# Scores and V products of an attention kernel tied into one run on TensorE

## The chip, the cores and the metric

The kernel runs on one core of a Trainium2 chip. The metric is the time of one execution on the device, in microseconds (us); the median of three runs of the kernel before is 1221.32 us (1220.86 to 1222.01). A core has TensorE (PE, matmuls, with its weight loads shown apart as PEld), VectorE (DVE), ScalarE (ACT), GpSimd (POOL) and SyncE (SP, which issues DMAs). Matmul results land in PSUM and are copied from there by DVE or ACT.

## What is computed

Attention over hash buckets, then a Fourier mix with a feed-forward layer (B = 4 batches, H = 8 heads, S = 768 positions, D = 64, model width 512, hidden width 2048):

```python
q_bits = (einsum('bhsd,dk->bhsk', q, proj) > 0)          # 6 bits, k_bits alike
mask = q_bucket[:, :, :, None] == k_bucket[:, :, None, :]
scores = where(mask, scale * matmul(q, k.transpose(0, 1, 3, 2)), -1e9)
attn = softmax(scores)                                   # over the keys
x = matmul(attn, v)                                      # -> (B, S, H*D)
mixed = real(fft(fft(x, axis=1), axis=2))
u = x + mixed
un = (u - mean(u)) / sqrt(var(u) + 1e-6)
out = u + maximum(un @ w_ch1, 0) @ w_ch2
```

All matmuls of scores, V products and layers are float32.

## The kernel before, in words

**Attention.** Heads are taken two at a time: a pair `n` (0 to 15, four to a batch) has its two heads in partitions 0 to 63 and 64 to 127. `attention(b)` (L851) goes over the four pairs of a batch, and for each over six chunks `c` of 128 keys. One chunk of one pair is called a step here; a step does the following.

- `weigh(n, g, c)` (L782), once for each query half `g` (384 queries): the two heads' scores go into one PSUM tile `sc` by two matmuls (L796), each with 64 rows, one on the upper and one on the lower half of the array. ACT takes the exponential into `pk` (L802), DVE multiplies it by the bucket mask, head by head (L805). So a step has four score matmuls: half 0 head 0, half 0 head 1, half 1 head 0, half 1 head 1. The profile shows two records for each float32 matmul, eight for a step. There are two `sc` tiles and four `pk` tiles.
- DVE adds `pk` into running sums (L876), once for each half.
- `finish()` (L855) then takes the step before out of the list `pending` and calls `values` (L811): four matmuls (L816), for each half two heads, whose results lie in partitions 0 to 63 and 64 to 127 of a PSUM tile `oo`. Behind a pair's last chunk comes `scale` (L821), with the sum matmuls (L833) and the division. What is still pending at the end of a batch is finished behind the loop (L888).
- From the second chunk on, one piece of `prepare(n + 1)` (L694) is made ready: transposes of q and k (L708), hash bits (L749), and for pairs 5 to 15 the bucket numbers of queries `qb` (L761, four bfloat16 matmuls) and keys `kb` (L770, six small ones), both through `sc` tiles. Pairs 0 to 4 are "lite": they have no `kb`, and take the mask through two further matmuls for each half, which add into the same scores (L791).

**The mix.** `mix(b)` makes the Fourier transforms (L964, L993), then in two halves of the positions the hidden layer `h` (L1018, chains of four matmuls over 384 columns, then a relu on ACT or DVE), transposes `un` (L1034), and the output `o` (L1049, chains of sixteen matmuls over 512 columns, added to `u` by DVE and stored). These use the two small PSUM tiles `ps`, in turn with the transposes, bits and sums of attention.

**Order.** Batch 0's attention stands in a `manual_schedule` block (L1080), in which PE, DVE, ACT and POOL keep the written order. From batch 1 on, attention of batch `b` is written step by step, with some pieces of the mix of batch `b - 1` behind every step (L1107 to L1113); batch 3's mix comes last, alone. There the order on each engine is left to the scheduler of the framework: it plays the program through and gives an engine, of the instructions that are ready, the one that ranks first; the rank is the written order unless the program raises it. A score matmul written behind h matmuls can so be started before them, when those wait for a PSUM tile.

Of the kernel before, what the change touches and what calls it, by code (L numbers as in the profile page):

```python
# [1 line left out]

# [1 line left out]

# [6 lines left out]
F32 = mybir.dt.float32  # L11
# [8 lines left out]
P = 128  # L20
# [4 lines left out]
NT = S // P  # L25
NPAIR = H // 2
HALF = S // 2
# [451 lines left out]
def _main(  # L479
# [13 lines left out]
    nc = tc.nc  # L493
# [13 lines left out]
    def wt(shape, dtype, tag, name, bufs=2):  # L507
        return work.tile(shape, dtype, tag=tag, name=name, bufs=bufs)
# [15 lines left out]
    def evac(dst, src, act=False):  # L524

        flip[0] ^= 1
        if flip[0] and not act:
            nc.vector.tensor_copy(dst, src)  # L528
        else:
            nc.scalar.copy(dst, src)  # L530
# [37 lines left out]
    pw = const.tile([P, 2, P], BF16, tag="pw", name="pw")  # L568
# [9 lines left out]
    for i in range(NPK):  # L578
        pk = const.tile([P, 2, HALF + 1], F32, tag=f"pk{i}", name=f"pk{i}")
# [114 lines left out]
    def prepare(n):  # L694

        lite = n in LITE
        act = lite and n > 0
        ts = {}  # L700
        for io, nm in enumerate("qk"):
            tn = nat.pop((nm, n))
            tt = wt([P, S], F32, nm + "t", f"{nm}t{n}")
            for g in range(2):
                ps = pt([P, 3, P], f"tr{nm}{n}_{g}")
                for i in range(3):
                    c = 2 * i + g if nm == "q" else 3 * g + i
                    nc.tensor.transpose(  # L708
                        ps[:, i, :], tn[:, c].rearrange("p h d -> p (h d)"), ident
                    )  # L710
                if nm == "q":
                    for i in range(2):
                        dst = tt[:, i * HALF + g * HALF // 2 : i * HALF + (g + 1) * HALF // 2]
                        evac(
                            dst.rearrange("p (j c) -> p c j", c=3),
                            ps[:, :, i * D : (i + 1) * D], act,
                        )
                else:
                    evac(
                        tt[:, g * HALF : (g + 1) * HALF],  # L720
                        ps.rearrange("p c t -> p (c t)"), act,
                    )
            ts[nm] = tt
            yield
            norm(n, io, tn)
        if lite:


            qk = wt([P, 2, S], BF16, "qb", f"qkb{n}")
            for io, nm in enumerate("qk"):  # L730
                for g in range(2):
                    cols = slice(g * HALF, (g + 1) * HALF)
                    ps = pt([P, HALF], f"bits{nm}{n}_{g}")
                    nc.tensor.matmul(ps, pjw, ts[nm][:, cols], start=True, stop=True)
                    bits = qk[:, io, cols]
                    nc.vector.tensor_scalar(
                        bits, ps, 0.0, off[:, io : io + 1],
                        op0=ALU.is_gt, op1=ALU.subtract,
                    )
                    if io == 0:  # L740
                        nc.vector.tensor_scalar(bits, bits, BIG, None, op0=ALU.mult)
                yield
            preps[n] = ts["q"], ts["k"], qk, None
            return

        ps = pt([P, HALF], f"bits{n}")
        for j in range(4):
            src = ts["qk"[j // 2]][:, (j % 2) * HALF : (j % 2 + 1) * HALF]
            nc.tensor.matmul(  # L749
                ps[32 * j : 32 * j + 32, :], pj, src, start=True, stop=True  # L750
            )
        bt = wt([P, HALF], BF16, "bt", f"bt{n}")
        nc.vector.tensor_scalar(bt, ps, 0.0, None, op0=ALU.is_gt)
        yield

        qb = wt([P, 2, S], BF16, "qb", f"qb{n}")
        for h in range(2):
            ps = ps_sc.tile([P, 2, 512], F32, tag="sc", name=f"qb{n}_{h}")
            for g in range(2):
                rows = slice(32 * g, 32 * g + 32)  # L760
                nc.tensor.matmul(  # L761
                    ps[:, g, 0:HALF], pw[rows, h, :], bt[rows, :], start=True, stop=True
                )
            evac(qb[:, h, :].rearrange("p (g s) -> p g s", g=2), ps[:, :, 0:HALF])
        kb = wt([P, 2, NT], F32, "kb", f"kb{n}")
        ps = ps_sc.tile([P, 2, 512], F32, tag="sc", name=f"kb{n}")
        for c in range(NT):
            g, i = divmod(c, NT // 2)
            rows = slice(64 + 32 * g, 96 + 32 * g)
            nc.tensor.matmul(  # L770
                ps[:, g, 2 * i : 2 * i + 2], bt[rows, i * P : (i + 1) * P],
                pw[rows, :, 0], start=True, stop=True,
            )
        nc.vector.tensor_copy(
            kb.rearrange("p h (g i) -> p g i h", g=2),
            ps[:, :, 0:NT].rearrange("p g (i h) -> p g i h", h=2),
        )
        preps[n] = ts["q"], ts["k"], qb, kb

    npk = [0]  # L780

    def weigh(n, g, c):  # L782

        qt, kt, qb, kb = preps[n]
        qs = slice(g * HALF, (g + 1) * HALF)
        ks = slice(c * P, (c + 1) * P)
        ps = ps_sc.tile([P, 2, 512], F32, tag="sc", name=f"sc{n}_{g}_{c}")
        heads = [slice(h * D, (h + 1) * D) for h in range(2)]
        if kb is None:
            for h, rows in enumerate(heads):  # L790
                nc.tensor.matmul(  # L791
                    ps[:, h, 0:HALF], qb[rows, 1, ks], qb[rows, 0, qs],
                    start=True, stop=False,
                )
        for h, rows in enumerate(heads):
            nc.tensor.matmul(  # L796
                ps[:, h, 0:HALF], kt[rows, ks], qt[rows, qs],
                start=kb is not None, stop=True,
            )
        pk = pks[npk[0] % NPK]  # L800
        npk[0] += 1
        nc.scalar.activation(pk[:, :, 0:HALF], ps[:, :, 0:HALF], AF.Exp, scale=SCALE)  # L802
        if kb is not None:
            for h in range(2):
                nc.vector.scalar_tensor_tensor(  # L805
                    pk[:, h, 0:HALF], qb[:, h, qs], kb[:, h, c : c + 1], pk[:, h, 0:HALF],
                    op0=ALU.is_equal, op1=ALU.mult,
                )
        return pk

    def values(n, c, pk, oos):  # L811

        for g in range(2):
            w = HALF + 1 - g
            for h in range(2):
                nc.tensor.matmul(  # L816
                    oos[g][h * D : (h + 1) * D, 0:w], nat["v", n][:, c, h, :],
                    pk[g][:, h, 0:w], start=(c == 0), stop=(c == NT - 1),
                )
# [31 lines left out]
    def attention(b):  # L851
        xs[b] = wt([P, NPAIR, S], F32, "x", f"x{b}")
        pending = []

        def finish():  # L855
            n, c, pk, oos, accs = pending.pop(0)
            values(n, c, pk, oos)
            if c == NT - 1:
                scale(n, oos, accs)

        for t in range(NPAIR):
            n = NPAIR * b + t
            half = fold(b, 0) if t == NPAIR - 1 else iter(())
            if 1 < n + 1 < NPAIR * B:
                load(n + 1)
            ahead = prepare(n + 1) if n + 1 < NPAIR * B else iter(())
            oos = [ps_o.tile([P, 512], F32, tag="o", name=f"oo{n}_{g}") for g in range(2)]
            accs = [wt([P, 2, HALF], F32, "t3", f"acc{n}_{g}", 4) for g in range(2)]
            first = None
            for c in range(NT):  # L870
                new = [weigh(n, g, c) for g in range(2)]
                if c == 0:
                    first = new
                else:
                    for g in range(2):
                        nc.vector.tensor_tensor(  # L876
                            accs[g], first[g][:, :, 0:HALF] if c == 1 else accs[g],
                            new[g][:, :, 0:HALF], op=ALU.add,
                        )
                while pending:  # L880
                    finish()
                pending.append((n, c, new, oos, accs))
                if c > 2:
                    next(half, None)
                if c > 0:
                    next(ahead, None)
                yield
        while pending:  # L888
            finish()

# [205 lines left out]
    for b in range(B):  # L1096
# [17 lines left out]
        if b == B - 1:  # L1114
# [6 lines left out]
            ps = pt([1, 3, P], "norms_t")  # L1121
# [65 lines left out]
```

## Time and profile before

| what | value |
|---|---|
| median of three runs | 1221.32 us |
| the profiled execution | 1220.78 us, span 1218.6 us |
| granted TensorE clock, mean | 0.994 of full speed |
| scores, L796, in all | 768 records, 187.3 us busy |
| V products, L816, in all | 768 records, 145.0 us busy |
| h, L1018, in all | 1024 records, 346.3 us busy |
| o, L1049, in all | 800 records, 339.9 us busy |
| mask multiplies, L805 | 264, 615 ns each |
| exponentials, L802 | 192, 809 ns each |

The span goes from the first to the last instruction of the profiled execution; the rest of its time lies around it. A row of a group has the line, the engine, the operation, what it writes and reads by the program's names, the shape and the count; then the busy time, the mean length of one in ns, and the idle time of the engine just before them with what ended it. A row of the timeline has the start, the length of a run of like instructions (to the end of the last, which can overlap the start of the next row), and their count; in brackets stands the engine's idle time before it. Where matmuls follow each other closely, the distance between starts is what they cost PE. A row of the waits has who waited for whom, the time in all, how often, and the longest.

### The profile page before, as it was taken

The numbers are of one execution on the slowest core, as the hardware profiler recorded it, in microseconds if no ns is written. First come the engines' busy times: TensorE is split into PE (matmuls) and PEld (weight loads), VectorE is DVE, ScalarE is ACT, GpSimd is POOL, SyncE is SP. The second block draws the span as 40 slices with busy tenths as digits, with TensorE's granted clock in tenths as the row PEclk, the third lists the DMA queues.
The fourth block names the chain that finished last, engine by engine and source line by source line (L and its number), as shares of the span: only waits on it lengthen the run. The fifth ranks groups of instructions, "written<-read, shape, count | busy, mean of one in ns | idle before, by whom it ended". The sixth has DMA issues, their size and how long they took to land. (4 is left out here: it accounts for less than half of the span.)

```text
span 1218.6 us, 11905 instructions
## 1 busy us (share of the span) xinstructions
PE 1182.9 (97%) x4617; PEld 596.3 (49%) x4617; DVE 635.4 (52%) x1202; ACT 347.0 (28%) x612; POOL 57.6 (5%) x128
## 2 busy tenths in 40 slices
PE   7999899999999999999999999999999999999997
PEld 4444364444444456454445445554445546654555
DVE  5889869753374547545446555655445753211110
ACT  7877356532132122222222213222122210000000
POOL 1000001000000010000000010000000000001001
PEclk9999999899999999999999999999999999999999
DMA  9522124201010010100101011010000000000000
GB/s 277 156 65 45 44 87 147 83 14 43 9 26 14 22 38 6 27 13 22 35 22 27 1 31 35 1 39 1 22 17 1 1 10 18 1 1 17 9 9 20
DMA packets 82896, 44.24 MB, mean 36 GB/s; under 512 B 76816, under 2 KB 76944, under 8 KB 82832
## 3 DMA queue, kind: packets, MB, share of 16 engines
q1 hardware_dynamic: 75600, 23.61, 8.0%
q0 software_dynamic: 5664, 19.40, 4.9%
q8 instruction: 38, 0.62, 0.2%
q10 hardware_dynamic: 1568, 0.39, 0.2%
q14 instruction: 26, 0.21, 0.1%
HBM read 37.10 MB, written 6.29 MB: 36 GB/s over the span
## 5 line engine op out<-in xcount | busy, mean ns | idle before, releaser
L1018 PE MATMUL h<-x,w 128*128 128x384 f32 x1024 | 346.3, 494 | 4.8 <-ACT qt L530 2.4
L1049 PE MATMUL o<-w,h 128*128 128x512 f32 (+1 forms) x800 | 339.9, 578 | 0.0
L1018 PEld LDWEIGHTS h<-x,w 128*128 128x128 f32 x1024 | 192.2, 191 | 150.8 <-issue 13.1
L805 DVE SCALAR_TENSOR_TENSOR pk<-qb,kb,pk 128x384 f32<-128x384 bf16 x264 | 151.2, 615 | 184.0 <-ACT pk L802 183.8
L1049 PEld LDWEIGHTS o<-w,h 128*128 128x128 f32 x800 | 148.3, 190 | 169.5 <-issue 160.3
L802 ACT ACTIVATE pk<-sc 128x768 f32<-128x768 f32 x192 | 148.4, 809 | 217.8 <-PE sc L796 178.7
L796 PE MATMUL sc<-qt,kt 64*128 64x384 f32 x768 | 187.3, 507 | 0.0
L816 PE MATMUL oo<-pk,vn 128*64 128x385 f32 (+1 forms) x768 | 145.0, 499 | 0.0
L876 DVE TENSOR_TENSOR acc<-acc,pk 128x768 f32<-128x768 f32 x128 | 120.4, 955 | 9.2 <-ACT pk L802 7.6
L1027 ACT ACTIVATE h<-h 128x384 f32<-128x384 f32 x64 | 31.4, 490 | 281.3 <-PE h L1018 281.2
L1025 DVE TENSOR_SCALAR h<-h 128x384 f32<-128x384 f32 x64 | 35.5, 554 | 143.0 <-PE h L1018 142.9
L796 PEld LDWEIGHTS sc<-qt,kt 64*128 64x128 f32 x768 | 76.6, 186 | 65.9 <-issue 44.3
L1055 DVE SCALAR_TENSOR_TENSOR u<-o,rs,u 128x512 f32<-128x512 f32 (+1 forms) x25 | 18.2, 729 | 165.8 <-PE o L1049 118.3
L816 PEld LDWEIGHTS oo<-pk,vn 128*64 128x64 f32 x768 | 46.6, 136 | 87.3 <-issue 82.5
L1036 ACT COPY u<-un 128x512 f32<-128x512 f32 x24 | 14.0, 586 | 127.3 <-PE un L1034 127.3
L1042 POOL TENSOR_SCALAR rs<-mv 128x1 f32<-128x1 f32 x24 | 7.7, 323 | 593.4 <-DVE mv L1040 588.4
L903 POOL DMA_DIRECT2D out_dram<-u x33 | 19.9, 603 | 316.4 <-DVE u L1055 255.7
L964 PE MATMUL cs<-ch,z 128*128 128x128 f32 (+3 forms) x192 | 31.1, 314 | 2.6 <-DVE kt L528 1.4
L964 PEld LDWEIGHTS cs<-ch,z 128*128 128x128 f32 x192 | 27.5, 191 | 10.1 <-DVE kt L528 3.1
L971 ACT COPY F<-cs 128x257 f32<-128x257 f32 (+1 forms) x32 | 11.1, 374 | 74.7 <-PE cs L964 74.7
L876 DVE TENSOR_TENSOR acc<-pk,pk 128x768 f32<-128x768 f32 x32 | 30.0, 951 | 2.0 <-ACT pk L802 1.7
L828 ACT ACTIVATE x<-oo,vs 128x384 f32<-128x384 f32 x32 | 16.8, 577 | 41.3 <-DVE vs L825 41.3
(107 smaller groups left out, 805.7 us busy)
## 6 DMA issues: line engine op xcount, KB each, us to landing
zraw<-in_moe_w_ch_dram POOLq DMA_DIRECT2D x21, 512.0 KB, 4.5
vn<-in_v_dram SPq DMA_DIRECT2D x32, 192.0 KB, 3.3
qn<-in_q_dram SPq DMA_DIRECT2D x31, 192.0 KB, 3.2
kn<-in_k_dram SPq DMA_DIRECT2D x31, 192.0 KB, 3.2
out_dram<-u POOLq DMA_DIRECT2D x15, 256.0 KB, 2.4
out_dram<-u POOLq DMA_DIRECT2D x18, 128.0 KB, 2.5
fraw<-in_moe_w_ch_dram SPq DMA_DIRECT2D x4, 512.0 KB, 9.2
fraw<-in_moe_w_ch_dram POOLq DMA_DIRECT2D x4, 512.0 KB, 4.5
```

What stands on the lines that cost most here:

```text
L796: nc.tensor.matmul(ps[:, h, 0:HALF], kt[rows, ks], qt[rows, qs], start=kb is not None, stop=True,)
L802: nc.scalar.activation(pk[:, :, 0:HALF], ps[:, :, 0:HALF], AF.Exp, scale=SCALE)
L805: nc.vector.scalar_tensor_tensor(pk[:, h, 0:HALF], qb[:, h, qs], kb[:, h, c : c + 1], pk[:, h, 0:HALF], op0=ALU.is_equal, op1=ALU.mult,)
L816: nc.tensor.matmul(oos[g][h * D : (h + 1) * D, 0:w], nat["v", n][:, c, h, :], pk[g][:, h, 0:w], start=(c == 0), stop=(c == NT - 1),)
L876: nc.vector.tensor_tensor(accs[g], first[g][:, :, 0:HALF] if c == 1 else accs[g], new[g][:, :, 0:HALF], op=ALU.add,)
L903: nc.gpsimd.dma_start(out[b, s0 : s0 + 2 * w - 1 : 2, cols], src[at : at + w, cols])
L964: nc.tensor.matmul(ps[:, pc + 2 * lo : pc + 2 * hi - 1 : 2], z[:, cp, pc, par, t * P : (t + 1) * P], ch[:, cp, pc, lo:hi], start=(cp == 0) ...
L1018: nc.tensor.matmul(ps, w1[:, c, fc * P : (fc + 1) * P], x[:, c, g * HALF : (g + 1) * HALF], start=(c == 0), stop=(c == NDC - 1),)
L1025: nc.vector.tensor_scalar(hr, ps, 0.0, None, op0=ALU.max)
L1027: nc.scalar.activation(hr, ps, AF.Relu)
L1049: nc.tensor.matmul(ps, hs[fc][:, j * P : (j + 1) * P], w2[:, fc, cols], start=(fc == 0), stop=(fc == NFC - 1),)
L1055: nc.vector.scalar_tensor_tensor(u[:, cols], ps, rs, u[:, cols], op0=ALU.mult, op1=ALU.add)
```

## The change

Two context managers are used together. `tc.issue_after(ins)` orders the matmuls made inside it behind `ins` on PE; `tc.high_priority(offset=500)` raises their rank by 500 places. `behind()` does both, behind the matmul that was noted last in `last[0]`. The rank of the first matmul of a step's scores stays as it was; the other three, each behind the one before, and then the four V products of the step before, all behind the last score matmul, are raised. This holds for batches 1 to 3 (`n >= NPAIR`), and not for the V products that are finished behind a batch's loop (`t is None`). The `qb` and `kb` matmuls are tied in the same way, and the tile `kb` is made before the `qb` matmuls instead of behind them. The instructions, their operands and the DMAs are the same.

```diff
         qb = wt([P, 2, S], BF16, "qb", f"qb{n}")
+        kb = wt([P, 2, NT], F32, "kb", f"kb{n}")
         for h in range(2):
...
-                nc.tensor.matmul(
-                    ps[:, g, 0:HALF], pw[rows, h, :], bt[rows, :], start=True, stop=True
-                )
+                with behind() if g + h else nullcontext():
+                    last[0] = nc.tensor.matmul(
+                        ps[:, g, 0:HALF], pw[rows, h, :], bt[rows, :],
+                        start=True, stop=True,
+                    )
             evac(qb[:, h, :].rearrange("p (g s) -> p g s", g=2), ps[:, :, 0:HALF])
-        kb = wt([P, 2, NT], F32, "kb", f"kb{n}")
...
+            with behind() if c else nullcontext():
+                last[0] = nc.tensor.matmul(
+                    ps[:, g, 2 * i : 2 * i + 2], bt[rows, i * P : (i + 1) * P],
+                    pw[rows, :, 0], start=True, stop=True,
+                )
...
+    AHEAD = 500
+
+    last = [None]
+
+    @contextmanager
+    def behind():
+
+        with tc.issue_after(last[0].ins), tc.high_priority(offset=AHEAD):
+            yield
...
         for h, rows in enumerate(heads):
-            nc.tensor.matmul(
-                ps[:, h, 0:HALF], kt[rows, ks], qt[rows, qs],
-                start=kb is not None, stop=True,
-            )
+            with behind() if g + h and n >= NPAIR else nullcontext():
+                last[0] = nc.tensor.matmul(
+                    ps[:, h, 0:HALF], kt[rows, ks], qt[rows, qs],
+                    start=kb is not None, stop=True,
+                )
...
             n, c, pk, oos, accs = pending.pop(0)
-            values(n, c, pk, oos)
+            with behind() if n >= NPAIR and t is not None else nullcontext():
+                values(n, c, pk, oos)
...
+        t = None
         while pending:
             finish()
```

More of the change, by code (lines that the diff above doesn't have):

```diff
@@ L1 @@
-from contextlib import ExitStack
+from contextlib import ExitStack, contextmanager, nullcontext
 import numpy as np
@@ L769, in prepare @@
             rows = slice(64 + 32 * g, 96 + 32 * g)
-            nc.tensor.matmul(
-                ps[:, g, 2 * i : 2 * i + 2], bt[rows, i * P : (i + 1) * P],
-                pw[rows, :, 0], start=True, stop=True,
-            )
+            with behind() if c else nullcontext():
[3 more added lines that the diff above has]
+                )
         nc.vector.tensor_copy(
@@ L795, in weigh @@
         for h, rows in enumerate(heads):
-            nc.tensor.matmul(
-                ps[:, h, 0:HALF], kt[rows, ks], qt[rows, qs],
-                start=kb is not None, stop=True,
-            )
+            with behind() if g + h and n >= NPAIR else nullcontext():
[3 more added lines that the diff above has]
+                )
         pk = pks[npk[0] % NPK]
```

## The prediction

> **What bounds the kernel now.** I read the page's busy line first, then the table of stages, then the waits of TensorE (PE).
>
> ```profile
> span 1218.6 us, 11905 instructions
> PE 1182.9 (97%) x4617; PEld 596.3 (49%) x4617; DVE 635.4 (52%) x1202; ACT 347.0 (28%) x612; POOL 57.6 (5%) x128
> ```
> ```profile
> 0.00:140.00 140.00, 124.76 (x658) 57.03 (x660) 112.90 (x207) 96.12 (x178) 6.49 (x28) 0.99 0.44 122
> 140.00:220.00 80.00, 74.14 (x363) 42.81 (x363) 63.58 (x125) 51.33 (x97) 7.40 (x14) 0.96 0.39 117
> 220.00:990.00 770.00, 763.09 (x2883) 370.04 (x2882) 414.16 (x776) 183.22 (x305) 29.46 (x56) 1.00 0.08 20
> 990.00:1219.00 229.00, 220.87 (x717) 126.40 (x715) 44.72 (x98) 16.29 (x34) 14.21 (x30) 0.99 0.04 11
> ```
>
> The columns after the length are busy time (and instructions) of PE, weight loads, DVE, ACT, POOL, then the granted clock. Batch 0, written out by hand, lies before 140 and is untouched; the last mix lies after 990, with no scores. The change works in 140 to 990. In 220 to 990 PE is idle for 6.9 us of 770, DVE for 356. So PE's own time sets the end there, and whatever PE no longer spends comes off the end, unless a wait appears.
>
> Is all that busy time needed? Scores (L796) and V products (L816) answer it. They have the same number of columns and the same kind of packing: two heads side by side, each on half the array.
>
> ```profile
> L796 PE MATMUL sc<-qt,kt 64*128 64x384 f32 x568 | 146.6, 516 | 0.0
> L816 PE MATMUL oo<-pk,vn 128*64 128x385 f32 x284 | 61.6, 512 | 0.0
> L816 PE MATMUL oo<-pk,vn 128*64 128x384 f32 x284 | 57.9, 486 | 0.0
> ```
>
> These are groups of 140 to 990: 568 records each way (a float32 matmul leaves two records, so one step has 8), but the scores take 146.6 us and the V products 119.5. The timeline of PE shows why.
>
> ```profile
> 594.74 0.91 PE L796 MATMUL sc<-qt,kt 64*128 64x384 f32 x2
> 595.58 7.13 PE L1049 MATMUL o<-w,h 128*128 128x512 f32 x16
> 602.65 1.55 PE L796 MATMUL sc<-qt,kt 64*128 64x384 f32 x6
> 604.13 1.51 PE L816 MATMUL oo<-pk,vn 128*64 128x385 f32 x8
> 605.57 0.52 PE L749 MATMUL bits<-qt,pj 128*32 128x384 f32 x2
> ...
> 613.42 1.56 PE L796 MATMUL sc<-qt,kt 64*128 64x384 f32 x8
> 614.91 1.51 PE L816 MATMUL oo<-pk,vn 128*64 128x385 f32 x8
> ```
>
> At 613.42 a step's scores run whole: 8 records, 1.49 us until V starts. At 594.74 the first head's matmul runs alone (2 records) and holds PE for 0.84 us until 595.58; its partner comes 7 us later, in a run of 6 that takes 1.48, as long as a whole run of 8: there the second head of half 0 shares the array with the first head of half 1, and the last head is alone. So the early piece is pure loss. The V products are never torn: 1.44 us each time.
>
> **The change, part by part.** *Lone heads.* I went along the PE timeline and sorted the 66 steps of pairs 5 to 15. 29 are whole. 26 are torn into 2 and 6 (first at 185.81, last at 976.17). 7 are in three pieces, as here:
>
> ```profile
> 410.28 0.91 PE L796 MATMUL sc<-qt,kt 64*128 64x384 f32 x2
> 411.12 0.66 PE L1034 MATMUL un<-ident,x 128*128 128x128 f32 x4
> 411.71 0.92 PE L796 MATMUL sc<-qt,kt 64*128 64x384 f32 x4
> 412.56 14.00 PE L1049 MATMUL o<-w,h 128*128 128x512 f32 x32
> ```
>
> A piece of 2 holds PE 0.84 us, a piece of 4 for 0.85. 4 steps are in two halves of 4. Whole, each would take 1.49. Saved: 26 x (0.84 + 1.48 - 1.49 = 0.83) = 21.6; 7 x (0.84 + 0.85 + 0.84 - 1.49 = 1.04) = 7.3; 4 x (2 x 0.85 - 1.49 = 0.21) = 0.8. Together 29.7 us.
>
> *Entering and leaving the packed form.* A long run of plain matmuls between plain neighbours gives the clean spacing:
>
> ```profile
> 1098.92 13.90 PE L1049 MATMUL o<-w,h 128*128 128x512 f32 x32
> 1112.66 0.60 PE L1034 MATMUL un<-ident,x 128*128 128x128 f32 x4
> ```
>
> 13.74 us for 32 records, 0.429 each. The 16 records between the two pieces at 595.58 and 602.65 took 7.07 us, where 16 x 0.429 is 6.87: each visit to packed matmuls costs the plain ones around it 0.20 us. The torn steps have 26 + 14 + 4 = 44 pieces too many; 9 pieces follow a sum matmul, whose own packed form pays this anyway. 35 x 0.20 = 7.0 us.
>
> Check against the group: 71 steps x 1.56 (a whole run's length above) = 110.8, against 146.6: 35.8 too much. My classes give 29.7 plus 44 x 0.07 (a piece's 0.91 overlaps the next by 0.07) = 32.8; the other 3 us are pair 4. There two further score matmuls per half (L791) aren't glued, only the heads: between 0 and 3 us, and I take 2, since the heads are most of it.
>
> *Waits behind torn scores.* Some pieces fill time in which PE would wait for a copy out of PSUM, and not all of it:
>
> ```profile
> PE h L1018 <- ACT qt L530: 2.4, 4, 0.6
> PE cs L964 <- ACT qt L530: 1.2, 2, 0.6
> ```
> ```profile
> 349.82 1.15 DVE L805 SCALAR_TENSOR_TENSOR pk<-qb,kb,pk 128x384 f32<-128x384 bf16 x2 [3.77 <-ACT pk L802]
> 351.69 1.55 PE L796 MATMUL sc<-qt,kt 64*128 64x384 f32 x6
> 351.88 1.14 DVE L805 SCALAR_TENSOR_TENSOR pk<-qb,kb,pk 128x384 f32<-128x384 bf16 x2
> 353.85 8.01 PE L1018 MATMUL h<-x,w 128*128 128x384 f32 x24 [0.60 <-ACT qt L530]
> ```
>
> Glued, the scores and V of this place last 1.49 + 1.44 = 2.93 us from 351.69, to 354.62, past the 353.85 at which h was free to go: these six waits (3.6 us) go under cover. Ends: 0 and 3.6; I take 3.6. The later gaps of such a step lose their filler, but the next step's run of 2.93 us can take it, since its first matmul keeps its old place.
>
> *The new wait.* The V products now come directly behind the next step's scores, and the transposes, h, o and bits matmuls queue behind them on PE; ACT and DVE (relu, copies out of PSUM, bits) wait for those. V needs the exponentials (ACT) and masks (DVE) of its own step. The tightest place is the one just shown: V would start at 351.69 + 1.49 = 353.18, and the last mask ends at 351.88 + 1.14 = 353.02. Twelve steps of pairs 5 to 15 follow the one before this closely. If V is put behind some h instead, it costs one more visit, 0.20 each, 2.4 us; if it fits, 0; if it falls apart into single heads, 2.7 each (rival 1), 32 us. I take 2.4, nearest to the row with its margin of 0.16.
>
> *The rest* costs nothing: qb and kb matmuls already run as 4 and 6 in a row; the earlier kb tile moves no instruction; no DMA is moved; batch 0 and the last V products of a batch are left as they are.
>
> *The early stage.* 140 to 220 has 5.9 us of idle PE, which I count at zero change; the low end takes it as covered, with what follows its longest wait:
>
> ```profile
> 214.20 8.15 PE L1018 MATMUL h<-x,w 128*128 128x384 f32 x15 [2.37 <-ACT kt L530]
> ```
> ```profile
> 214.00:221.00 7.00, 6.80 (x12) 3.81 (x13) 4.95 (x10) 6.61 (x14) 0.53 (x1) 0.54 0.60 185
> ```
>
> After a wait of 2.37 us the granted clock was 0.54 for 7 us, another 7 x 0.46 = 3.2 us. The Trainium skill (TensorE: Matmul & The Clock Gate, Part 1) lets the clock fall only after an idle window of about 3.4 us; by it this wait would cost nothing more and the low end would be 3 us higher. The trace contradicts that here, and a row decides.
>
> *Sum.* 29.7 + 7.0 + 2 + 3.6 - 2.4 = 39.9 us. The profiled execution took 1220.78 (span 1218.6 and 2.2 around it), 0.5 under the median of 1221.32. 1220.8 - 39.9 + 0.5 = 1181.4, so 1181.
>
> **The rivals.** *1. V waits for DVE and falls apart: slower.* The V matmuls are raised in rank one by one and not tied to each other. Where a step's run comes before the masks are done, each head may go as its mask comes, with plain matmuls between. No lone V head is in the trace; the nearest row is a lone score head, 0.84 plus 0.20 for the visit: four make 4.2 us, against 1.44 in the run, 2.7 us lost per step. The gain of 39.9 is gone from 15 steps on. At two steps of each of the 12 pairs, 24 x 2.7 = 65: 1246 us. For it: DVE's masks of half 1 wait for the half-0 sum, and only 0.16 us is to spare at 353.18. Against: only twelve steps are this close, and DVE is 54% busy (414 of 770). Chance 6%. The Trainium skill (TensorEngine Tiling, PSUM Bottleneck) warns that packing speeds TensorE and not the evacuation, which may then set the pace; this is that rule at work, and DVE's share speaks against it so far.
>
> *2. The pieces were fillers, and the waits come back.* If the next run can't take a gap, PE idles for what 353.85 shows still left, about 0.6 us, at most of the 35 plain pieces: 35 x 0.6 = 21, so 1202 us. For it: the pieces stand behind transposes and sums, which fill both small PSUM buffers. Against: the run is longer than any piece, there are 72 of them, and the 9 pieces behind sums need little (h follows at once). 10%.
>
> *3. The glue doesn't bind.* If being ordered behind a matmul isn't being next to it, the pieces stay: 1221 us. Against: accumulating matmuls, too, are only ordered one behind the other, and run unbroken: 32 records of o at 412.56, two chains of 16. 4%.
>
> **How the numbers follow.** Forecast 80%, rivals 10, 6 and 4. The forecast's own range goes from 1181 less 5.9 + 3.2, that is 1172, to 1181 plus the 5.6 of the two terms taken at their good ends and a third of rival 1's twelve steps (11), 1198. To hold rival 2, it reaches to 1204. A measurement of this kernel can tell about 0.2%, 2.4 us, from no change. Faster by more: 80 + 10 + 1 of rival 1's few-step form = 91%; within: 3; slower: 5 of rival 1 and 1 of rival 3 = 6.
>
> **What would show it.** Right: nearly every row of L796 between 140 and 990 with x8 and a V row x8 directly behind; their group at 111 to 115 us instead of 146.6, V still near 119.5; the plain matmul groups unchanged in busy time but for the visits; PE idle no more than 10 us. Wrong, by rival 1: V rows of x2 or x4, and V's group well over 120. By 2: the scores at 111, but waits of h, o and transposes on ACT or DVE above 15 us in sum. By 3: scores at 146 still. The forecast is wrong if the time is above 1204 with scores whole.

## The result, and the profile after

The changed kernel takes 1189.1 us (median of 4, 1188.4 to 1190.8) against 1221.7: a ratio of 0.974, 95% interval 0.972 to 0.975. Its profiled execution took 1188.4 us. First the page's head:

```profile
span 1186.2 us, 11922 instructions
PE 1148.7 (97%) x4617; PEld 585.8 (49%) x4617; DVE 634.2 (53%) x1202; ACT 346.0 (29%) x612; POOL 60.2 (5%) x128
```

The span is 32.4 us shorter, PE's busy time 34.2. So PE is idle for 37.5 us (span less busy), 1.8 more than before: the gain is all in PE's busy time, and waits took back a little of it. Now the groups of 140 to 990, as shown of before (busy us and mean ns, then idle us before them; L811 and L831 are the score and V lines of the changed kernel):

```profile
L811 PE MATMUL sc<-qt,kt 64*128 64x384 f32 x568 | 111.7, 507 | 0.0
L831 PE MATMUL oo<-pk,vn 128*64 128x385 f32 x288 | 64.2, 512 | 0.5 <-DVE pk L820 0.4
L831 PE MATMUL oo<-pk,vn 128*64 128x384 f32 x288 | 59.4, 487 | 0.0
```

Scores fell from 146.6 to 111.7 us for the same 568 records. V has 8 records more in this window; in the whole program V went from 145.0 to 147.0. The timeline of PE shows the runs:

```profile
641.40 0.49 PE L708 MATMUL trk<-ident,kn 128*128 128x128 f32 x3
641.82 1.56 PE L811 MATMUL sc<-qt,kt 64*128 64x384 f32 x8
643.31 1.51 PE L831 MATMUL oo<-pk,vn 128*64 128x385 f32 x8
644.75 0.55 PE L708 MATMUL trk<-ident,kn 128*128 128x128 f32 x3
645.14 7.91 PE L1035 MATMUL h<-x,w 128*128 128x384 f32 x24
652.97 0.52 PE L749 MATMUL bits<-qt,pj 128*32 128x384 f32 x2
...
653.75 5.43 PE L1035 MATMUL h<-x,w 128*128 128x384 f32 x16
```

Of the 66 steps of pairs 5 to 15, 64 have their scores whole, 2 in halves; no lone score head is left. Two things differ from what the prediction drew. The raised run cuts the six transposes of k into 3 and 3. And the bits matmuls, which in the kernel before stood right behind V (605.57 there) and shared its packed form, now stand alone between plain matmuls (652.97), another visit.

At two steps V fell apart as rival 1 has it, in the crowded stretch around 200 us:

```profile
195.17 1.56 PE L811 MATMUL sc<-qt,kt 64*128 64x384 f32 x8
196.66 2.20 PE L1035 MATMUL h<-x,w 128*128 128x384 f32 x6
198.92 0.86 PE L831 MATMUL oo<-pk,vn 128*64 128x385 f32 x2
199.71 0.91 PE L1035 MATMUL h<-x,w 128*128 128x384 f32 x2
200.55 0.86 PE L831 MATMUL oo<-pk,vn 128*64 128x385 f32 x2
201.34 0.91 PE L1035 MATMUL h<-x,w 128*128 128x384 f32 x2
202.18 0.87 PE L831 MATMUL oo<-pk,vn 128*64 128x384 f32 x4
```

A lone V head (2 records) holds PE for 0.79 us, until 199.71. Between 220 and 990 the h matmuls wait like this; the row below the waits is one of the two places:

```profile
PE h L1035 <- ACT qt L530: 2.3, 2, 1.3
PE h L1035 <- DVE h L1042: 1.1, 1, 1.1
```
```profile
352.92 1.88 PE L1035 MATMUL h<-x,w 128*128 128x384 f32 x5 [1.28 <-ACT qt L530]
```

The four waits of h of 0.6 us are gone, but two longer ones of the same kind (up to 1.3 us) came with the cut transposes: their second half, and so its copies on ACT, comes behind the run.

### The profile page after: what moved, and what is told of

The parts are those of the page before. It is cut to its first block, busy times and chain, and to the rows that moved or that the text cites. A ratio compares the mean times of both kernels' runs of the same rounds, so it can differ in the third digit from the quotient of the medians.

```text
span 1186.2 us, 11922 instructions
## 1 busy us (share of the span) xinstructions
PE 1148.7 (97%) x4617; PEld 585.8 (49%) x4617; DVE 634.2 (53%) x1202; ACT 346.0 (29%) x612; POOL 60.2 (5%) x128
## 5 line engine op out<-in xcount | busy, mean ns | idle before, releaser
L817 ACT ACTIVATE pk<-sc 128x768 f32<-128x768 f32 x192 | 147.2, 809 | 149.0 <-PE sc L811 111.7
L811 PE MATMUL sc<-qt,kt 64*128 64x384 f32 x768 | 152.4, 501 | 0.0
L831 PE MATMUL oo<-pk,vn 128*64 128x385 f32 (+1 forms) x768 | 147.0, 499 | 0.5 <-DVE pk L820 0.4
L831 PEld LDWEIGHTS oo<-pk,vn 128*64 128x64 f32 x768 | 47.0, 136 | 88.7 <-issue 71.3
L811 PEld LDWEIGHTS sc<-qt,kt 64*128 64x128 f32 x768 | 67.0, 187 | 45.0 <-issue 23.0
L981 PE MATMUL cs<-ch,z 128*128 128x128 f32 (+3 forms) x192 | 31.3, 316 | 2.5 <-DVE kt L528 1.3
```

Source lines behind the costliest of these rows:

```text
L811: last[0] = nc.tensor.matmul(ps[:, h, 0:HALF], kt[rows, ks], qt[rows, qs], start=kb is not None, stop=True,)
L831: nc.tensor.matmul(oos[g][h * D : (h + 1) * D, 0:w], nat["v", n][:, c, h, :], pk[g][:, h, 0:w], start=(c == 0), stop=(c == NT - 1),)
L981: nc.tensor.matmul(ps[:, pc + 2 * lo : pc + 2 * hi - 1 : 2], z[:, cp, pc, par, t * P : (t + 1) * P], ch[:, cp, pc, lo:hi], start=(cp == 0) ...
```

## The experiments

The theory: PE's time is the bound, and what counts is how scores and V are packed. It gives a price list: from the trace of before, a lone score head 0.84 us, a piece of two paired heads 0.85, a whole run of scores 1.49, of V 1.44, and 0.20 for each visit to packed matmuls; from the trace of after, a lone V head 0.79. With the pieces counted in the order of a kernel's instructions, before has 46 lone score heads and 137 visits, the changed kernel none and 114. (Counted from the start of the traces the visits are 144 and 121, the same 23 apart.) The rivals: what pays is V standing right behind the scores; or pieces cost little, since they fill waits. All ratios are against the kernel before on the same chip.

**One part at a time.** In the first kernel only the second head is tied behind the first:

```diff
-            with behind() if g + h and n >= NPAIR else nullcontext():
+            with behind() if h and n >= NPAIR else nullcontext():
...
-            with behind() if n >= NPAIR and t is not None else nullcontext():
+            with nullcontext():
                 values(n, c, pk, oos)
```

(and no ties for qb and kb, as in the next two). The expectation on record:

> Only the second head of each half is tied behind the first; halves, V products and qb/kb are left alone. Theory (PE's packed time pays: a lone head's piece 0.84 us, a piece of two paired heads 0.85, a whole run 1.49, 0.20 for each visit): no lone score heads, but 138 half pieces of 4 records and 27 whole runs, counted in the order of its instructions; scores 24 us less than before, three V runs torn 2 us more, as many visits as before: 22 us off, 1200 us. Rival (what pays is V right behind the scores, and the visits shared): little of it is here, 1212 or more.

Measured: 1195.1 us, ratio 0.978 (0.976 to 0.980). That is 5 us under the expected 1200: the score and V groups (below) moved as expected, 24.1 us down and 2.6 up, and 2.1 us of the rest are idle time of PE (33.6 against 35.7); what is left over stays open. The second kernel ties all four score matmuls, and not V:

```diff
-            with behind() if n >= NPAIR and t is not None else nullcontext():
+            with nullcontext():
                 values(n, c, pk, oos)
```

> All four score matmuls of a step tied, V products and qb/kb left alone. Theory: scores whole as in the changed kernel (32 us), but V stands apart in more steps and is torn in seven places: 5.6 us back, 5 visits fewer than before; 28 us off, 1194 us, so that tying V is worth 5 us of the 32. Rival (V right behind the scores pays): 1205 or more.

Measured: 1193.0 us, 0.977 (0.975 to 0.979). The third ties V alone:

```diff
-            with behind() if g + h and n >= NPAIR else nullcontext():
+            with nullcontext():
                 last[0] = nc.tensor.matmul(
```

> Only the V products are tied behind the step's last score matmul and raised; scores and qb/kb are left alone. Theory: the scores stay torn (48 lone pieces), V mostly stood behind them already: 1222 us, no change within 2 us. Rival (V right behind the scores pays): 1206 or less.

Measured: 1218.5 us, 0.998 (0.997 to 0.999), 2.4 us under before. The score and V groups of the whole program, for the first and then the second of these kernels (the order of the page's costliest groups):

```profile
L811 PE MATMUL sc<-qt,kt 64*128 64x384 f32 x768 | 163.2, 513 | 0.0
L831 PE MATMUL oo<-pk,vn 128*64 128x384 f32 (+1 forms) x768 | 147.6, 499 | 0.0
```
```profile
L811 PE MATMUL sc<-qt,kt 64*128 64x384 f32 x768 | 151.8, 500 | 0.0
L831 PE MATMUL oo<-pk,vn 128*64 128x384 f32 (+1 forms) x768 | 151.1, 500 | 0.0
```

and of the third:

```profile
L811 PE MATMUL sc<-qt,kt 64*128 64x384 f32 x768 | 188.2, 507 | 0.0
```

Before has 187.3 and 145.0, the changed kernel 152.4 and 147.0. Keeping heads together is worth 26 us of the 32; tying the halves takes the scores down by another 11 us, but V, left alone, is torn and stands apart, 151.1, so only 2 us are left of that, and the ranges of the two kernels overlap (1192.8 to 1197.3, 1191.9 to 1194.0); tying V as well gives the last 4. V alone moves no more than 2 to 3 us, and its scores are as torn as before. Even that need not come from V: the median granted clock of its ten executions was 0.998, against 0.996 in the thirteen of before, and 0.002 of 1219 us is 2.4. The rival that V's place is what pays falls.

**Ties without rank.** The whole change with `AHEAD = 0`:

```diff
-    AHEAD = 500
+    AHEAD = 0
```

> The whole change, but the raise in rank set from 500 to 0: the ties give the order only. Theory: scores are torn as before, and V, tied behind a matmul but ranked by its place, comes apart too: 123 lone V heads, 236 visits to packed matmuls instead of 137. With 0.79 to 0.84 us for a lone head and 0.20 for a visit, 80 us more than before: 1300 us. Rival (torn pieces cost little by themselves, the time lies in waits): under 1240.

Measured: 1291.4 us, 1.058 (1.056 to 1.060): slower by 70 us, where the price list says 80. The page's head, its V group, and a stretch of its timeline:

```profile
span 1289.7 us, 11899 instructions
PE 1264.2 (98%) x4617; PEld 605.6 (47%) x4617; DVE 638.8 (50%) x1202; ACT 349.7 (27%) x612; POOL 57.1 (4%) x128
```
```profile
L831 PE MATMUL oo<-pk,vn 128*64 128x384 f32 (+1 forms) x768 | 206.0, 507 | 0.0
```
```profile
622.96 0.86 PE L831 MATMUL oo<-pk,vn 128*64 128x385 f32 x2
623.75 0.33 PE L708 MATMUL trk<-ident,kn 128*128 128x128 f32 x1
624.01 0.87 PE L831 MATMUL oo<-pk,vn 128*64 128x385 f32 x4
624.80 0.33 PE L708 MATMUL trk<-ident,kn 128*128 128x128 f32 x1
```

V comes in pieces of 2 and 4 between single transposes, and takes 206.0 us instead of 145.0. The price of rival 1, a V run in pieces, is thus shown: PE's busy time rose by 81.3 us (1264.2 against 1182.9). Its mechanism isn't, since here V falls apart for want of rank and not because DVE's masks are late. The 10 us that the list has too much are PE's idle time: 25.5 us (span less busy) against 35.7 before. So pieces do fill waits, and give back about an eighth of what they cost (10 of 80). That rival is right in kind and small in size.

**A smaller raise**, `AHEAD = 60`:

> The whole change with the raise in rank set from 500 to 60. Counted in the order of its instructions: 23 lone score heads are left of 46, 33 lone V heads come in, and visits to packed matmuls rise from 137 to 161. Theory (the pieces' prices alone): 0.1 us less than before: 1221 us, the gain gone though the ties are all there. Rival (the tie, not the raise, does it; torn pieces hide in waits): 1189 to 1200 us.

Measured: 1215.4 us, 0.996 (0.994 to 0.997). Nearly the whole gain is gone, far from the rival's 1200; but the list is 5 us off. PE is idle for 33.4 us, 2.3 less than before. The other 3 us are of the size of a difference in the clock: the median granted clock of these executions was 0.997, and 0.995 in those of before, which is 2.4 of 1215 us.

**Ties of qb and kb.** The change without them, the `with behind()` around both replaced by `nullcontext()`:

> The change without the ties of the qb and kb matmuls. Its order on TensorE is the changed kernel's, instruction by instruction, so by the theory 1189 us, within 2 us of it; a rival by which these ties pay would show it slower by more.

Measured: 1189.6 us, 0.974 (0.973 to 0.976), the changed kernel's own. These ties do nothing.

**Can the shortfall be had back?** Four kernels on one chip, five rounds each. First the changed kernel:

> The changed kernel once more, to stand beside the next three on one chip: 1189 us by either theory.

Measured: 1188.8 us (1187.5 to 1191.7). Then V turned round:

```diff
-        for g in range(2):
+        for g in (1, 0):
             w = HALF + 1 - g
-            for h in range(2):
+            for h in (1, 0):
+                with behind() if tie else nullcontext():
+                    last[0] = nc.tensor.matmul(
...
```

Here `tie` is the condition that stood around `values` (`n >= NPAIR and t is not None`), so that each V matmul is now tied behind the one before it.

> The change, with the four V products in the opposite order, each tied behind the one before: the head whose mask comes last goes first, so the other three can't start ahead of it. Theory: the V runs that the change tears (three lone heads, a run of two, a run of three around 200 us) come whole, 1.8 us, and 3 visits go, 0.6 us: 2.4 us off, 1187 us, V's spacing back to that of before. Rival (V's masks are the limit there, so PE waits instead of tearing): 1189, with the time as idle PE before V.

Measured: 1187.4 us (1186.9 to 1189.4). The ranges overlap, so a gain of 1.4 us isn't certain; at the same granted clock of 0.998 the two took 1187.5 and 1186.9. The page's V row and the waits of this kernel:

```profile
L832 PE MATMUL oo<-pk,vn 128*64 128x384 f32 (+1 forms) x768 | 145.0, 499 | 2.8 <-DVE pk L820 2.0 <-ACT x L844 0.8
```
```profile
PE oo L832 <- DVE pk L820: 2.0, 5, 0.7
```

V's busy time is back to the 145.0 of before, and 2.0 us of waits for the masks came in its place, which the changed kernel has for only 0.4: in the crowded stretch the masks are the limit, and torn or whole, V pays for them. In the two profiles with the changed kernel's and this order, PE's busy time fell by 2.1 us (1148.7 to 1146.6) and its idle time rose by 1.5. The theory was right on the pieces, the rival on most of the time.

Then also the preparation of pairs 5 to 15 one chunk later:

```diff
-                if c > 0:
+                if c > (n + 1 not in LITE):
                     next(ahead, None)
```

> As the one before, and the pieces of the next pair's preparation come one chunk later (pairs 5 to 15). Theory: 108 visits instead of 111, 0.6 us off: 1186 us, if no wait takes its place. Rival (visits cost nothing by themselves): as the one before; if the masks' bucket numbers come too late for the next pair, slower than it by 1 to 3 us, as idle PE before V.

Measured: 1184.4 us (1184.1 to 1184.7), 0.970 (0.969 to 0.971). All its runs lie under all of the other three kernels': the fastest version here, 4 us under the changed kernel. The three fewer visits explain 0.6 of the 3 us to the kernel with V turned round; PE's idle time fell by 1.8 us (1181.9 - 1144.7 = 37.2 against 1185.6 - 1146.6 = 39.0); the rest I didn't separate.

Last, scores that can't fill gaps:

```diff
-            with behind() if g + h and n >= NPAIR else nullcontext():
+            with (behind() if g + h and n >= NPAIR else
+                  tc.issue_after(lastt[0].ins) if n > NPAIR else nullcontext()):
```

where `lastt[0]` is the transpose of q or k (L708) written last; V is turned round here too, and the preparation stands where the changed kernel has it.

> As the kernel with the V products turned round, and each step's first score matmul is also ordered behind the transposes written before it, so that scores can't fill the gaps ahead of those (runs of sums, then h, then transposes). Packed time by the pieces: 0.4 us less than there. Theory with fillers of no worth: 1187 us. Rival 2 of the prediction (the scores filled waits, and these come back): PE idle 5 to 10 us above that of the changed kernel, 1192 to 1197 us.

Measured: 1197.7 us (1196.6 to 1199.7), 10 us over the kernel with V turned round, with the same pieces and two visits fewer. So where a step's scores start matters: they cover waits. From the timeline of this kernel, and the windows (the last three columns are the granted clock, the DMA share and GB/s):

```profile
188.06 2.32 PE L1013 MATMUL A<-sq,F 128*128 128x193 f32 x8 [2.25 <-DVE rt L858]
191.85 2.90 PE L1013 MATMUL B<-sq,F 128*128 128x193 f32 x8 [1.47 <-DVE x L1029]
...
212.22 2.57 PE L1038 MATMUL h<-x,w 128*128 128x384 f32 x4 [2.28 <-ACT h L1047]
```
```profile
188.00:193.00 5.00, 3.47 (x12) 3.00 (x13) 4.51 (x11) 0.00 (x0) 0.00 (x0) 0.57 0.00 0
...
213.00:220.00 7.00, 6.75 (x25) 3.36 (x25) 4.10 (x8) 5.85 (x12) 1.06 (x2) 0.78 0.74 219
```

PE's idle time is 42.2 us, 3.2 more than with V turned round. Its busy time is 7.9 us more, with the same work: behind these waits the clock was 0.57 and 0.78, and the mean granted clock of the execution was 0.992, against 0.999 with V turned round, which is 8 of 1197 us. So these waits were paid for twice, as idle time and as slower matmuls behind them. Rival 2 of the prediction has its mechanism, though the change itself doesn't set it off: it left each step's first score matmul at its old rank.

## Why the prediction was right, and by how much it missed

It said 1181, with 1172 to 1204; it was 1189. The forecast case happened: 32.4 us of 39.9. Point by point, with PE's time summed from the starts of its 4617 records, idle time apart:

- *Lone heads and halves, 29.7 us, and pair 4, 2 us.* Score records cost 173.0 us before and 141.3 after: 31.7, of which 30.1 in pairs 5 to 15 and 1.7 in pair 4. As predicted.
- *Visits, 7.0 us.* This step failed. I counted the 35 pieces that would go, and not what would lose its neighbour. Visits fell from 137 to 114 only, 23 rather than 35: bits (8 places) and qb (7), which had followed V within the same visit, are now alone. Plain records next to packed ones cost 27.2 us before beyond the spacing that they have among their like, and 23.5 after (slowed stretches of the clock left out); bits and qb of pairs 5 to 15 cost 0.3 more. About 3.4 us are left of the 7.
- *Waits behind torn scores, 3.6 us.* This failed too. The waits at these places went, as argued, and others came, of h behind cut transposes and in the stretch around 190 us: PE idle rose by 1.8 us, instead of falling by 3.6. I took the good end because the run covers the old wait; it also moves the work that the next wait is for.
- *The new wait, 2.4 us.* V's records cost 2.1 us more (137.1 to 139.3). Right in size, by luck: the 2.4 stood for V behind some h, one visit each at twelve close steps. What came is V in pieces at two steps around 200 us, as rival 1 has it, and at 643.31 and its like V runs whole behind the scores.
- *The early stage, zero.* In the profiled execution of before the clock fell in 214 to 221, in that of after not: 15 records of h took 8.15 us there (the prediction's row at 214.20), where 16 take 5.43 at 653.75, some 3 us. It also fell before 140, at 126 to 133 (0.76), some 1 us; and four matmul records of hash bits at 8 to 11 us, where the change does nothing, cost 1.1 us more after. Together some 3 us of the gain of this pair of profiles are that. Whether it is chance isn't shown: where both kernels ran side by side, the median granted clock was 0.995 before and 0.997 after.
- *Plain matmuls among plain ones, not in the sum.* They cost 2.9 us more than before (1.1 of it h), the slowed stretches and those bits left out. What causes it stays open.

So 39.9 less 3.6, less 5.4, 0.3 and 3 more, and less 2.9: 31.3, against the 32.4 of the spans. The mechanism was right, and the two missed terms are both of one kind: the order that the change makes elsewhere. Rival 1 came true in a stretch of 13 us (198.92 to 211.6), where DVE is behind (busy for all of the 7 us from 194 on), and nowhere else. The prediction set beside it a rule of the Trainium skill (TensorEngine Tiling, PSUM Bottleneck) on the copies out of PSUM; what V waits for here is the masks, which DVE multiplies into `pk` after ACT has read PSUM, so these two steps are no case of that rule.

## What to carry to other kernels

Where two half-array matmuls share TensorE, a scheduler that sees them as independent can start one as a gap filler and lose the partner: compare the busy time of the group with that of a like group that runs whole, and price pieces by the distance of starts. Tie the partners first; that alone gave four fifths of the gain here. A tie that gives only the order makes things worse without the rank to go with it, and whatever used to stand next to the tied run must be counted too.

## What was not expected of the hardware

The same wait in the same program did not always cost the clock. The changed kernel waits 2.91 us for DVE before a group of eight matmuls, in both of its profiled executions. The first, then the second, each with the window behind the wait:

```profile
193.66 1.57 PE L1010 MATMUL B<-sq,F 128*128 128x193 f32 x8 [2.91 <-DVE rt L854]
194.00:201.00 7.00, 6.95 (x28) 3.37 (x26) 7.00 (x17) 4.27 (x9) 1.05 (x2) 1.00 0.32 109
```
```profile
195.85 2.62 PE L1010 MATMUL B<-sq,F 128*128 128x193 f32 x7 [2.91 <-DVE rt L854]
196.00:203.00 7.00, 7.00 (x24) 4.25 (x24) 5.90 (x15) 3.39 (x7) 0.53 (x1) 0.80 0.34 118
```

Eight records took 1.57 us in one, seven took 2.62 in the other; the granted clock over the 7 us behind the wait was 1.00 (194 to 201) and 0.80 (196 to 203). The Trainium skill (TensorE: Matmul & The Clock Gate, Part 1) says that the window in which idleness is judged runs free of the program, which would make it chance whether a wait falls into one window; these two agree with that, though at 2.9 us and not at the 3.4 it gives. The two executions differ by 3.5 us of span with the same work, and their mean granted clock was 0.998 and 0.995, which is 3.6 of 1190 us. The times of this kernel on one chip follow the clock as well: 1187.5 and 1187.7 us at 0.998, 1188.8 at 0.997, 1190.7 and 1191.7 at 0.995. So look at the granted clock before reading a term of 2 us from one pair of profiles.
